# A new hand-written instruction order for a one-core attention and feed-forward kernel

## The chip, the core and the metric

The kernel runs on one core of a Trainium2 chip. The metric is the device time of one execution in microseconds (us). Five instruction streams run side by side and meet only at semaphores: TensorE (matmuls), ScalarE (activations), VectorE, GpSimd, and SyncE, which here only issues DMA transfers.

## The reference

```
xn  = layernorm(x)                      # x: 2048 x 640
q   = (xn @ wq) as 32 heads of 20       # one k and one v head for all
p   = softmax(q k^T / sqrt(20))         # 2048 x 2048 for each head
out = x + (p v) @ wo + silu(xn @ w1) @ w2      # w1: 640 x 1728
```

All inputs and the output are bf16.

## The kernel before

**Tiling.** The 2048 queries are four chunks of 512; the 32 heads are eight groups of four, each head in a strip of 32 partitions. A chunk and a group of heads make one of 32 *groups*, numbered chunk by chunk. In a group, each of 16 key tiles of 128 keys gives four *score blocks* of 128 x 512, one for each head: 2048 blocks in all. A score matmul uses 32 rows of the array, so up to four on different row strips run side by side; such a *score set* takes the time of one matmul. The product with v uses 32 columns for each head: a *value group* is four matmuls of 512 columns side by side.

**Two ways to the exponential.** ScalarE takes a run of one to three neighbouring PSUM banks in one exp (L1258). VectorE takes single blocks: p1 (L1503) turns a score into the bit pattern of an approximate exponential, and two shifted copies of the four blocks of a batch sharpen it, made by GpSimd (L1542) or by VectorE (L1547). A key tile of ScalarE's thus costs one value group, a batch of VectorE's three (all at L1295).

**Dense work.** The projections q, the feed-forward's first layer h (with a tanh on ScalarE, L863, and a product on VectorE, L866), the output jobs ("out", with the second layer and wo) and those of the last chunk ("y", "fin") are jobs of 5 to 19 steps on TensorE (L537, L824), four matmuls side by side in each. Queries are spread into the head strips by small DMAs, the query pieces (L796). When a group ends, its denominators travel through three DMA steps (L938, L943, L946), GpSimd multiplies (L950), and DMAs pack the rows for wo (L963). An output job of a chunk needs the packed rows of all eight groups of it. The h jobs of chunks 2 and 3 need output jobs of chunks 0 and 1 to be done.

**Who sets the order.** The whole program is laid out ahead of time by a planner in the source, class `Sched` with `build`: each operation has an assumed duration and a priority, and `commit` gives it its place on its engine. Up to an assumed 36 us (`HAND`) the planner itself chooses. From there TensorE's order is read from the text `ORDER`, three characters for each step, by `follow`:

- `S`: a score run for ScalarE (banks, first bank); `s` the same, but it begins a new set
- `D`, `E`: one score block for VectorE (batch and head, bank); with `E` the batch's shifts may go to VectorE; `F`, `G` the same, beginning a new set
- `a`, `d`: one value group of a ScalarE tile or of a VectorE batch
- `n`: the first step of a dense job (`q`, `h`, `o`, `y`); `m`: its next step

The texts in `OTHERS` give the order on ScalarE, VectorE and GpSimd, and who goes first at the port which the last two share. SyncE's queue of DMAs is not in them: there the planner takes the transfer with the lowest `prio` among those that it thinks ready. When `ORDER` is used up, the planner goes on by itself. The assumed times set the order only; on the chip each engine runs its list in this order, waiting on semaphores.

## Time and profile before

| | |
|---|---|
| median of three runs | 681.21 us (680.39 to 681.31) |
| profiled execution, its own time | 681.22 us |
| its span, first to last instruction | 679.4 us |
| TensorE busy | 666.0 us, 98% |
| ScalarE busy | 654.4 us, 96% |
| VectorE busy | 632.2 us, 93% |
| GpSimd busy | 514.1 us, 76% |
| mean granted TensorE clock | 0.995 |

Busy times overlap: an instruction's time on an engine runs from its start to its end, and the next may start before that end. Rows by stretch give, for each engine, busy time and in brackets the number of instructions, then the granted clock, the share of the DMA engines and GB/s.

### The profile page before, as it was taken

How to read it: one execution, taken by the hardware profiler on the slowest of the kernel's cores; microseconds unless marked ns; L12 is line 12 of the kernel's file. 1: busy time of each engine (PE TensorE's matmuls, PEld its weight loads, DVE VectorE, ACT ScalarE, POOL GpSimd, SP SyncE). 2: the span in 40 equal slices, each digit the busy share in tenths (PEclk: the TensorE clock that was granted, in tenths of full speed). 3: DMA queues.
4: the chain of work that ended last, by engine and by line, in shares of the span. 5: the costliest groups of instructions: out<-in, count | busy, mean ns of one | idle time of the engine just before them, and what ended most of it. 6: DMA issues, size and time to landing. Idle time of an engine off the chain costs nothing.

```text
span 679.4 us, 22817 instructions
## 1 busy us (share of the span) xinstructions
PE 666.0 (98%) x9898; PEld 240.8 (35%) x9901; DVE 632.2 (93%) x1102; ACT 654.4 (96%) x728; POOL 514.1 (76%) x314
## 2 busy tenths in 40 slices
PE   8999999999999999999999999999999999999998
PEld 5433323332322333333333333333332333333345
DVE  7899999999998999899999999999999899999943
ACT  6999999999998999999999999999999899999992
POOL 6648787878886887876888787788888857777760
PEclk9999999999998999999999999999999899999999
DMA  8652220222221223231212222312222202233201
GB/s 224 184 180 18 32 24 14 27 26 22 34 32 24 32 30 42 29 57 25 23 27 35 36 26 34 40 31 50 21 19 35 25 20 33 31 49 43 23 7 41
DMA packets 34243, 29.00 MB, mean 43 GB/s; under 512 B 15486, under 2 KB 29662, under 8 KB 34142
## 3 DMA queue, kind: packets, MB, share of 16 engines
q1 hardware_dynamic: 33854, 27.20, 25.9%
q8 instruction: 78, 1.28, 0.8%
q10 hardware_dynamic: 288, 0.33, 0.1%
q14 instruction: 23, 0.19, 0.1%
HBM read 11.09 MB, written 2.62 MB: 20 GB/s over the span
## 4 chain that ended last, share of the span: by engine, by line
PE 63%; ACT 20%; DVE 13%; POOL 3%; issue 1%; DMA 0%; POOLq 0%; ACTq 0%
PE psall L1295 21%; PE psall L1168 20%; PE psall L537 20%; ACT sbt L1258 18%; DVE sbt L1503 7%; POOL sbt L1542 3%; ACT sbt L863 1%; DVE sbt L1547 1%; DVE sbt L866 1%; DVE sbt L653 1%; DVE sbt L697 0%; DVE sbt L655 0%; PE psall L711 0%; DVE sbt L783 0%; DVE sbt L1344 0%
## 5 line engine op out<-in xcount | busy, mean ns | idle before, releaser
L1258 ACT ACTIVATE sbt<-psall 128x1024 bf16<-128x1024 f32 (+2 forms) x656 | 624.4, 1067 | 7.1 <-PE psall L1168 5.7
L1542 POOL TENSOR_SCALAR sbt<-sbt 128x2048 int16<-128x2048 int16 x238 | 451.5, 1897 | 112.3 <-PE psall L1295 40.9
L1503 DVE TENSOR_SCALAR sbt<-psall 128x512 int16<-128x512 f32 x712 | 454.6, 682 | 20.3 <-PE psall L1168 15.2
L1295 PE MATMUL psall<-sbt 128*32 128x512 bf16 x3472 | 273.6, 386 | 2.1 <-DVE sbt L1547 0.8
L1168 PE MATMUL psall<-sbt 32*128 32x512 bf16 x2048 | 255.8, 386 | 4.4 <-ACT sbt L1258 1.0
L537 PE MATMUL psall<-sbt 128*32 128x320 bf16 (+3 forms) x3900 | 218.9, 332 | 0.4 <-DVE sbt L1503 0.2
L1168 PEld LDWEIGHTS psall<-sbt 32*128 32x128 bf16 x2048 | 69.3, 91 | 225.6 <-ACT sbt L1258 125.6
L537 PEld LDWEIGHTS psall<-sbt 128*32 128x32 bf16 (+1 forms) x3900 | 84.2, 96 | 86.8 <-issue 46.6
L1295 PEld LDWEIGHTS psall<-sbt 128*32 128x32 bf16 x3472 | 72.8, 95 | 109.2 <-issue 70.6
L1547 DVE TENSOR_SCALAR sbt<-sbt 128x2048 int16<-128x2048 int16 x118 | 80.8, 710 | 0.6 <-PE psall L1295 0.5
L950 POOL TENSOR_TENSOR sbt<-sbt 128x512 bf16<-128x512 f32 x30 | 38.5, 1284 | 20.2 <-DVE sbt L1547 16.8
L866 DVE SCALAR_TENSOR_TENSOR sbt<-sbt,psall 128x512 bf16<-128x512 bf16 x52 | 35.1, 677 | 0.1
L863 ACT ACTIVATE sbt<-psall 128x512 bf16<-128x512 f32 x52 | 32.1, 619 | 0.0
L1344 DVE COPY sbt<-psall 128x512 f32<-128x512 f32 x31 | 21.1, 681 | 0.4 <-PE psall L1295 0.3
L783 DVE TENSOR_SCALAR sbt<-psall 128x512 bf16<-128x512 f32 x20 | 13.6, 678 | 0.1
L1009 DVE SCALAR_TENSOR_TENSOR sbt<-psall,sbt 128x320 f32<-128x320 f32 x8 | 3.9, 486 | 10.2 <-PE psall L537 10.2
L662 POOL TENSOR_TENSOR sbt<-sbt 128x2 f32<-128x2 f32 x8 | 5.7, 708 | 8.5 <-DVE sbt L660 8.2
L993 DVE SCALAR_TENSOR_TENSOR sbt<-psall,sbt 128x320 bf16<-128x320 f32 x24 | 11.6, 485 | 0.2 <-PE psall L537 0.2
L675 POOL TENSOR_SCALAR sbt<-sbt 128x640 bf16<-128x640 bf16 x12 | 10.4, 874 | 1.5 <-DVE sbt L667 1.5
L653 DVE BATCH_NORM_STATS2 sbt<-sbt 128x6 f32<-128x320 bf16 x14 | 6.6, 472 | 1.9 <-DMA sbt<-in_A_x_dram 1.9
L685 PE MATMUL psall<-sbt 128*128 128x128 bf16 x80 | 6.9, 220 | 1.5 <-DVE sbt L678 1.5
L1824 PE MATMUL psall<-sbt 128*32 128x256 bf16 x144 | 6.5, 338 | 1.2 <-DVE sbt L577 1.2
(63 smaller groups left out, 98.8 us busy)
## 6 DMA issues: line engine op xcount, KB each, us to landing
sbt<-sbt SPq DMA_DIRECT2D x120, 64.0 KB, 3.8
sbt<-in_A_x_dram SPq DMA_DIRECT2D x28, 160.0 KB, 4.1
sbt<-sbt SPq DMA_DIRECT2D x213, 20.0 KB
out_dram<-sbt SPq DMA_DIRECT2D x14, 160.0 KB, 2.1
sbt<-in_B_w_dram SPq DMA_DIRECT2D x1, 2160.0 KB, 13.9
sbt<-in_B_w_dram SPq DMA_DIRECT2D x1, 2080.0 KB, 8.4
sbt<-sbt SPq DMA_DIRECT2D x75, 8.0 KB
sbt<-in_A_wq_dram SPq DMA_DIRECT2D x1, 800.0 KB, 5.8
```

What stands on the lines that cost most here:

```text
L537: ins = pe.matmul(ps[j * SLOT:(j + 1) * SLOT, b * BANK + off:b * BANK + off + n], w[:, j * SLOT:(j + 1) * SLOT], x, start=start, stop=stop ...
L783: op = Op("dve", lambda v: v.tensor_scalar_mul(q_st[:, st, :], bk(job.bank), QSCALE), t_dve(512), DVE_END, pre=[job.ready], writes=[res("q ...
L863: t = Op("act", lambda a: a.activation(t_buf[0:rows, ts, :], bk(job.bank, 0, QW, rows=rows), AF.Tanh, scale=0.5), t_act(512), ACT_END, pre ...
L866: u = Op("dve", lambda v: v.scalar_tensor_tensor(out=hT[par][0:rows, fk, :], in0=t_buf[0:rows, ts, :], scalar=1.0, in1=bk(job.bank, 0, QW, ...
L950: nm = pool(lambda e: e.tensor_tensor(oU[:, us, :], U_sb[:, us, :], Rrep, ALU.mult), 1356.0, POOL_END, pre=[uc] + lc + pack_op.get(divmod( ...
L1168: return pe.matmul(bk(b), kT_rep[i * SLOT:(i + 1) * SLOT, kt * P:(kt + 1) * P], qT[i * SLOT:(i + 1) * SLOT, g % NQ, :], start=True, stop=T ...
L1258: return a.activation(Ebuf[:, es * QW:es * QW + w], ps[:, buf[0] * BANK:buf[0] * BANK + w], AF.Exp, scale=ESCALE)
L1295: ins = pe.matmul(ps[i * SLOT:(i + 1) * SLOT, ub * BANK:ub * BANK + QW], lhsT, rhs, start=(first and k < HG), stop=(last and k >= len(lst) ...
L1344: return v.tensor_copy(U_sb[:, us, :], bk(ub))
L1503: p1 = Op("dve", lambda v: v.tensor_scalar(z16[:, i * QW:(i + 1) * QW], bk(job.bank), ZBIAS, 0.0, ALU.add, ALU.max), t_dve(QW) + 2.0, DVE_ ...
L1542: op = pool(lambda v, t=t, j=j, zin=zin: v.tensor_scalar(t.bitcast(I16), zin, float(SHIFT[j]), 1.0, ALU.add, ALU.mult), POOL_SHIFT, POOL_E ...
L1547: op = dve(lambda v, t=t, j=j, zin=zin: v.tensor_scalar_add(t.bitcast(I16), zin, float(SHIFT[j])), t_dve(N, 4), prio=SPRIO - 0.01 * j, **args)
```

## The change

`ORDER` and the four texts of `OTHERS` are replaced as a whole. `ORDER` grows from 3046 to 3153 entries and reaches further into the program's end. Packed rows get a lower priority number in SyncE's queue. Three assumed durations of `make_sel`, which writes constants for the end of the program, are changed. An `S` entry can name banks with a step of two.

```diff
 ORDER = (
-    "D32D13S14a97nq6m00m00D25S20Dd2m00m00S23nh5aa7S20D66m00D32D03S14m00m00m00S20S12Dd6ab7nh4m00m00m00m00S20D33D05nh6m00m00m00m00nh2S20D23Dd4m00m00m00m00ac7"
...
-    "d94d84ny2m00m00S25E37m00S20Dc3m00da4d74dc4S35D33m00m00m00m00a54S10E21m00a64S35D33m00m00m00m00db4S20D13m00m00m00S25D87a74a84S30E23a94df4S35")
+    "D32D13S14a97nq6m00m00D25S20m00m00S22D34aa7S20Dd5nh6m00D04D22S13m00m00m00S20S14Dd5G33nh2m00m00m00m00S25D00D31nh4m00m00m00m00ab7S25D20S13nh2m00m00m00m00"
...
+    "S24D83m00m00m00dd7de7a00S31a10m00m00S24D17m00m00m00m00m00m00S21D33m00a20S24D27m00a30m00d00S31d30d10d60a40S35a50a60d20S31d40a70S35S14d50d70d90d80a80da0"
+    "S31db0S35")
...
                 o = dma(f"pk{us}", lambda e, c=c, r=r, n=n, lo=lo: e.dma_start(oT[r:r + n, par, c, :], oU[lo:lo + n, us, :]),
-                        n * QW * 2 + 200000, pre=[nm] + ([kT_op[k] for k in range(KT)] + q_op[0] if qc == 1 else []), reads=[res("oU", us)], writes=[res("oT", par, gi, i, c)], prio=0.6)
+                        n * QW * 2 + 200000, pre=[nm] + ([kT_op[k] for k in range(KT)] + q_op[0] if qc == 1 else []), reads=[res("oU", us)], writes=[res("oT", par, gi, i, c)], prio=0.45)
...
-        a = pool(lambda g: g.memset(qT[:, 2, :], 0.0), 300, writes=q_res[NGR - NQ] + [res("sel")], prio=0.91)
+        a = pool(lambda g: g.memset(qT[:, 2, :], 0.0), 1067, writes=q_res[NGR - NQ] + [res("sel")], prio=0.91)
...
         if k == "S":
-            op = make_s_act(tuple(range(b, b + int(a))))
+            d, n = divmod(int(a, 36), 4)
+            op = make_s_act(tuple(range(b, b + (n or 4) * (d + 1), d + 1))[:n or 4])
             what = ("s", None)
```

The two other durations of `make_sel` go from 180 to 193 and from 280 to 292. For reference, query pieces have `prio=0.55` and the three denominator steps `prio=0.5`.

## The prediction

> **What bounds the kernel now.** I read the page first, then the busy time by stretch, the groups by form, and the timelines of single engines.

> ```profile
> PE 666.0 (98%) x9898; PEld 240.8 (35%) x9901; DVE 632.2 (93%) x1102; ACT 654.4 (96%) x728; POOL 514.1 (76%) x314
> PE 63%; ACT 20%; DVE 13%; POOL 3%; issue 1%; DMA 0%; POOLq 0%; ACTq 0%
> 36.80:176.00 139.20, 138.50 (x1852) 44.47 (x1848) 137.45 (x232) 138.98 (x168) 110.76 (x61) 1.00 0.24 35
> 176.00:216.00 40.00, 37.39 (x430) 11.21 (x426) 38.52 (x63) 37.98 (x40) 32.49 (x18) 0.96 0.25 33
> 216.00:516.00 300.00, 299.16 (x4520) 104.00 (x4516) 289.48 (x485) 299.19 (x337) 239.99 (x133) 1.00 0.25 32
> 516.00:536.00 20.00, 18.50 (x213) 5.62 (x209) 18.15 (x31) 17.97 (x20) 17.57 (x13) 0.91 0.25 31
> 664.20:679.40 15.20, 11.88 (x315) 8.46 (x311) 5.64 (x11) 3.26 (x4) 0.00 (x0) 1.00 0.14 46
> ```

> Two engines bound it together: from 36.8 us on, TensorE and ScalarE are both busy for nearly the whole of most stretches (299.16 and 299.19 of 300 us), and DMA has 0% of the chain that ended last. The stretches 176 to 216 and 516 to 536 stand out: there both lose time, and the granted clock falls below 1. The opening up to 36.8 us is not in the hand-written order and stays.

> TensorE's prices come from its timeline (start, duration, then the matmuls):

> ```profile
> 565.52 0.39 PE L1168 MATMUL psall<-sbt 32*128 32x512 bf16 x3
> 565.84 0.40 PE L1295 MATMUL psall<-sbt 128*32 128x512 bf16 x4
> 566.17 0.39 PE L1168 MATMUL psall<-sbt 32*128 32x512 bf16 x3
> 566.50 0.73 PE L537 MATMUL psall<-sbt 128*32 128x320 bf16 x16
> 567.05 0.39 PE L1295 MATMUL psall<-sbt 128*32 128x512 bf16 x4
> 569.78 0.83 PE L1295 MATMUL psall<-sbt 128*32 128x512 bf16 x12
> 570.54 0.39 PE L1168 MATMUL psall<-sbt 32*128 32x512 bf16 x3
> ```

> Starts count, not durations. Four groups of 320 columns take 566.50 to 567.05, 0.136 each. A score set (L1168) followed by a value group (L1295) takes 0.32, and so does the way back, 0.33. Three value groups and one way back take 0.76 (569.78 to 570.54). From the last two, two more value groups cost 0.43, so 0.216 each, and a change between score and other work costs 0.105 on top, in either direction. There are no gaps: with the order given, TensorE's time is a sum of these.

> ScalarE likewise:

> ```profile
> L1258 ACT ACTIVATE sbt<-psall 128x1024 bf16<-128x1024 f32 x520 | 494.9, 1049 | 6.6 <-PE psall L1168 5.7
> L1258 ACT ACTIVATE sbt<-psall 128x1536 bf16<-128x1536 f32 x80 | 116.1, 1485 | 0.2
> L1258 ACT ACTIVATE sbt<-psall 128x512 bf16<-128x512 f32 x56 | 34.8, 632 | 0.3
> 311.68 1.49 ACT L1258 ACTIVATE sbt<-psall 128x1536 bf16<-128x1536 f32 x1
> 313.01 0.65 ACT L863 ACTIVATE sbt<-psall 128x512 bf16<-128x512 f32 x1
> 313.49 2.00 ACT L1258 ACTIVATE sbt<-psall 128x512 bf16<-128x512 f32 x2
> ```

> From start to start, three banks take 1.33 us and one bank 0.48; two banks lie between, an estimate of 0.905. Every exp thus carries about 0.05 us beside its elements.

> **The clock.** These windows of 3.41 us are laid on the two half-clock periods:

> ```profile
> 185.53:188.94 3.41, 2.93 (x26) 0.97 (x26) 3.41 (x7) 3.41 (x5) 2.97 (x3) 1.00 0.59 66
> 206.02:209.43 3.41, 2.23 (x21) 0.58 (x21) 3.41 (x5) 3.41 (x4) 1.56 (x1) 1.00 0.11 27
> 209.43:212.84 3.41, 3.35 (x31) 0.71 (x31) 2.64 (x5) 1.67 (x2) 2.57 (x2) 0.50 0.10 24
> 526.87:530.28 3.41, 2.33 (x25) 0.65 (x24) 3.40 (x6) 3.41 (x4) 3.12 (x3) 1.00 0.10 24
> 530.28:533.70 3.42, 3.42 (x34) 1.04 (x34) 1.71 (x3) 1.62 (x3) 3.18 (x4) 0.50 0.07 14
> ```

> In each half-clock window TensorE is busy throughout and ScalarE falls to 1.67 and 1.62 us: it loses 1.74 and 1.80 us, and TensorE half of 3.4. I take 1.75 us a period. The window ahead of each held the fewest matmuls of the steady part (x21, x25); a window of x26 passed. Every matmul here covers a quarter of the array, so the count is a measure of array work. I read it so: a sparse window halves the next one's clock. The sparse places are the two in which no dense work is to be had: after the last q and h job of one query chunk, until its output jobs may start. [...]

> **The change, part by part.** The order is a text of three-character entries; I count them by kind in its old and new form.

> ```profile
> L1295 PE MATMUL psall<-sbt 128*32 128x512 bf16 x3472 | 273.6, 386 | 2.1 <-DVE sbt L1547 0.8
> L1503 DVE TENSOR_SCALAR sbt<-psall 128x512 int16<-128x512 f32 x712 | 454.6, 682 | 20.3 <-PE psall L1168 15.2
> L1542 POOL TENSOR_SCALAR sbt<-sbt 128x2048 int16<-128x2048 int16 x238 | 451.5, 1897 | 112.3 <-PE psall L1295 40.9
> ```

> Score blocks: 2048 in all. The old order places 1255 in S entries and 705 in D and E entries, and leaves 88 to the opening and the planner's own end; the new places 1286 and 712, leaving 50, which is just the opening's share (46 and 4). So the new order runs to the last score block. VectorE now gets 716 blocks, 179 batches, against 712 (L1503 above), 178; ScalarE gets 1332 against 1336.

> *TensorE.* A batch adds two value groups: 868 (3472 by 4) become 870, +0.43 us. Walking the entries with the rule that neighbouring score blocks on different row groups share one set, I find 608 sets after the opening against 613, -1.08, and some 12 fewer changes between score and other work (about 1145 against 1157), -1.26. Dense jobs are the same. Sum -1.9 us, of some 640.

> *ScalarE.* Runs of one, two and three banks: 56, 520, 80 become 80, 506, 80. That is 24 x 0.48 - 14 x 0.905 = -1.2 us.

> *VectorE and GpSimd.* Four more p1 of 0.682 and two fewer shifts there; GpSimd four more shifts of 1.897, +7.6 us. Both are under 97% in 216 to 516, so I cost them at nothing; without that cover GpSimd's 7.6 would lie open.

> *Where dense work stands.* In the first sparse place the old order has two q jobs (10 groups, 40 matmuls) between the end of group 6 and the first output job, the new one (20): thinner. In the second, after group 23, the old has two q jobs; the new opens six h jobs in group 24, drawn from groups 21 and 22. Laying the entries along ScalarE's prices, I find the old order's sparse windows at about 187, 205 and 525 us, as the trace has them, and in the new one only the one near 205 falls under 24 matmuls a window. So the second half-clock period should go, -1.75 us; the first stays, or is missed if the windows fall otherwise (another -1.75).

> *The DMA queue.* Packed rows get priority 0.45 in place of 0.6: ahead of query pieces (0.55) and of the denominator's transfers (0.5), where both are ready.

> ```profile
> 185.34 6.75 SPq L796 DMA_DIRECT2D sbt<-sbt  x9
> 192.14 0.71 SPq L963 DMA_DIRECT2D sbt<-sbt  x1
> POOL sbt L950 <- DMA sbt<-sbt: 2.3, 3, 1.6
> ```

> Here packs (L963) do follow nine query pieces (L796). But the first output matmul comes only at about 213 us, and query pieces are placed several groups ahead of their first score, so either can slip by these 6.75 us unseen. The longest wait of the multiply on a transfer is 1.6 us. I cost the queue at 0, with bounds of -2.3 (all of that wait) and +2.3. The three changed durations of make_sel and the two-step stride of an S entry move nothing themselves; no S entry of the new order uses a stride.

> *The end.*

> ```profile
> 639.46 27.34 ACT L1258 ACTIVATE sbt<-psall 128x1024 bf16<-128x1024 f32 x23
> 667.08 2.07 PE L537 MATMUL psall<-sbt 128*32 128x320 bf16 x56
> 669.08 1.05 PE L1089 MATMUL psall<-sbt 128*128 128x4 f32 x8
> 670.97 5.11 PE L537 MATMUL psall<-sbt 128*32 128x128 bf16 x144
> ```

> The last exp ends at 666.80; from there 12.6 us pass, 2.07 of them on y jobs left over and about four on the parts of the last projection that need not wait. The new order has all y jobs placed before the last score set, and the early parts can run under the last exps. From the exps' side that saves up to 2.1 us; from TensorE's side nothing, for the same work is only moved, and the sums of group 30, earlier spread among score sets, now lie there too. I take 0, with -2.1 and +2 (the wait for the last exps lying open, about one run and a half of 1.33) as ends.

> *Sum.* Other waits, for which I have no ground to expect a change, are carried over. TensorE: -1.9 - 1.75 = -3.65; ScalarE: -1.2 - 1.75 - up to 2.1 = -5.05. The slower of the two counts. The profiled execution took 681.22 us around a span of 679.4 (1.8 outside it); the median is 681.21, so nothing is to be shifted. 681.2 - 3.65 is 677.6; with an even chance that the first half-clock period is missed too I lower it by a part of that, to **677.2 us**. This case alone: 675 to 679.

> **The rivals.** *The end eats it.* The cover of y jobs is gone, TensorE stands in wait of the last exps (+2 us) and the sparse places give two periods again: 681.2 - 1.9 + 2 = 681.3, no change. For it: the last entries are long runs on ScalarE with little between them. Against: the last projection's early parts are there to fill.

> *Short runs starve ScalarE: slower.* The 24 further one-bank runs give TensorE 0.48 us to bring the next score set, less than a change to other work and back with one group in between (0.32 + 0.33).

> ```profile
> 294.52 1.10 ACT L1258 ACTIVATE sbt<-psall 128x512 bf16<-128x512 f32 x2
> 295.74 0.60 ACT L1258 ACTIVATE sbt<-psall 128x512 bf16<-128x512 f32 x1
> ```

> Here two one-bank exps took 1.22 us from start to start of the third, where 0.96 would do: 0.26 lost. If every added one lost that, 24 x 0.26 = 6.2: 677.2 + 6.2 = 683.4. It decides from 0.22 us each. For it: the trace's own example, and 0.621 busy for each (34.8 by 56). Against: most one-bank runs stand ahead of a tanh of an h job, which fills the time.

> *The clock is no matter of sparse windows.* Then two periods stay: 681.2 - 1.9 = 679.3, still faster, by little.

> *The change does only half of what it says,* the queue's new priority moving nothing that anyone waits for: I hold this true, and it is in the sum.

> **How the numbers follow.** Forecast 0.56; end eats it 0.13; short runs or like waits in TensorE's fixed order 0.17; clock unchanged 0.10; better than the forecast, both periods gone and the end's 2.1 saved (673.8), 0.04. A measurement of this kernel can tell 0.2%, 1.4 us, from no change: faster means under 679.8, slower over 682.6. The forecast, the better case and most of the clock case are faster: 0.69; same 0.14; slower 0.17. The range, 673.8 to 682.5, leaves out most of the slower rival and little else.

> **What would show it.** Right: 870 value groups; exps 80, 506, 80; one half-clock period or none, none near 530; no y matmul after the last exp; matmul starts still 0.32 apart at each change. Wrong: two or more half-clock periods, or new ones; ScalarE below 99% in 216 to 516 with waits on L1168; more than 12.6 us from the last exp to the end; a TensorE wait on a transfer.

## The result, and the profile after

The changed kernel takes 675.01 us in the median of four runs (674.64 to 675.24); the kernel before took 680.8 us beside it (678.86 to 681.31). The ratio is 0.992, with a 95% interval of 0.9899 to 0.9941. The profiled execution of the changed kernel took 674.64 us around a span of 672.8 us, 6.6 us less than the span of 679.4 us before. Its line numbers are three higher: the exp is L1261, value groups are L1298, score matmuls L1171, p1 L1506, GpSimd's shift L1545, dense steps L540, packs L966.

From the page of the changed kernel, busy times and the chain by engine:

```profile
PE 662.0 (98%) x9911; PEld 241.6 (36%) x9911; DVE 628.5 (93%) x1102; ACT 653.1 (97%) x738; POOL 525.2 (78%) x320
PE 85%; DVE 10%; ACT 3%; issue 1%; POOL 1%; DMA 0%; DVEq 0%; ACTq 0%
```

The same stretches, by the view of windows (busy time and count for TensorE, its weight loads, VectorE, ScalarE and GpSimd; then granted clock, DMA share, GB/s):

```profile
36.80:176.00 139.20, 138.76 (x1858) 44.91 (x1854) 138.16 (x234) 139.11 (x173) 112.65 (x62) 1.00 0.24 35
176.00:216.00 40.00, 37.66 (x466) 11.96 (x465) 39.73 (x68) 40.00 (x41) 32.64 (x19) 1.00 0.26 32
216.00:516.00 300.00, 299.53 (x4512) 104.44 (x4512) 291.59 (x491) 299.58 (x337) 249.30 (x137) 1.00 0.27 34
516.00:536.00 20.00, 19.77 (x298) 6.72 (x294) 19.35 (x33) 19.76 (x24) 18.35 (x13) 1.00 0.16 17
```

The clock is 1.00 in every one: the two half-clock periods are both gone from this execution, and the other three have a mean clock of 0.999 or 1.0 too. ScalarE is busy for 40.00 us of 176 to 216, where it had 37.98, and for 19.76 of 516 to 536, where it had 17.97. In 216 to 516 it stays full. TensorE now holds 85% of the chain that ended last, where it had 63% and ScalarE 20%.

The groups by form show that the order says what was read from its text:

```profile
L1261 ACT ACTIVATE sbt<-psall 128x1024 bf16<-128x1024 f32 x506 | 483.0, 1061 | 2.3 <-PE psall L1171 1.9
L1545 POOL TENSOR_SCALAR sbt<-sbt 128x2048 int16<-128x2048 int16 x244 | 462.9, 1897 | 97.2 <-DVE sbt L1550 36.8 <-PE psall L1298 22.4 <-PE psall L1171 9.8
L1506 DVE TENSOR_SCALAR sbt<-psall 128x512 int16<-128x512 f32 x716 | 454.8, 681 | 21.0 <-PE psall L1171 16.9
L1298 PE MATMUL psall<-sbt 128*32 128x512 bf16 x3480 | 272.9, 384 | 1.4 <-POOL sbt L1545 1.1
L1261 ACT ACTIVATE sbt<-psall 128x1536 bf16<-128x1536 f32 x80 | 116.7, 1474 | 0.9 <-PE psall L1171 0.4
L1261 ACT ACTIVATE sbt<-psall 128x512 bf16<-128x512 f32 x80 | 49.2, 633 | 0.3 <-PE psall L1171 0.2
```

3480 matmuls make 870 value groups; the exps are 80, 506 and 80. ScalarE's waits at the three forms add to 3.5 us; they were 7.1 (6.6, 0.2 and 0.3).

The end, from the timelines of ScalarE and TensorE (start, duration, then what ran):

```profile
654.53 7.31 ACT L1261 ACTIVATE sbt<-psall 128x1536 bf16<-128x1536 f32 x6
...
661.89 0.40 PE L1298 MATMUL psall<-sbt 128*32 128x512 bf16 x4
662.12 0.40 PE L540 MATMUL psall<-sbt 128*32 128x128 bf16 x16
662.78 1.05 PE L1092 MATMUL psall<-sbt 128*128 128x4 f32 x8 [0.26 <-ACT sbt L1399]
664.66 4.88 PE L540 MATMUL psall<-sbt 128*32 128x128 bf16 x128
```

The last exp ends at 661.84, 10.96 us ahead of the end; before it was 12.6 us. The 2.07 us of y steps that lay there are gone, and only 16 of the last projection's 144 matmuls run ahead of the last sum.

### The profile page after: what moved, and what is told of

The parts are those of the page before. It is cut to its first block, busy times and chain, and to the rows that moved or that the text cites. A ratio compares the mean times of both kernels' runs of the same rounds, so it can differ in the third digit from the quotient of the medians.

```text
span 672.8 us, 22813 instructions
## 1 busy us (share of the span) xinstructions
PE 662.0 (98%) x9911; PEld 241.6 (36%) x9911; DVE 628.5 (93%) x1102; ACT 653.1 (97%) x738; POOL 525.2 (78%) x320
## 4 chain that ended last, share of the span: by engine, by line
PE 85%; DVE 10%; ACT 3%; issue 1%; POOL 1%; DMA 0%; DVEq 0%; ACTq 0%
PE psall L1298 29%; PE psall L1171 28%; PE psall L540 25%; DVE sbt L1506 7%; ACT sbt L1261 2%; DVE sbt L1550 1%; PE psall L714 1%; PE psall L688 1%; DVE sbt L869 0%; PE psall L827 0%; DVE sbt L1347 0%; DMA sbt<-in_A_x_dram 0%; PE psall L1110 0%; POOL sbt L1545 0%; DVE sbt L786 0%
## 5 line engine op out<-in xcount | busy, mean ns | idle before, releaser
L1261 ACT ACTIVATE sbt<-psall 128x1024 bf16<-128x1024 f32 (+2 forms) x666 | 624.4, 1059 | 3.5 <-PE psall L1171 2.5
L1545 POOL TENSOR_SCALAR sbt<-sbt 128x2048 int16<-128x2048 int16 x244 | 462.9, 1897 | 97.2 <-DVE sbt L1550 36.8
L1506 DVE TENSOR_SCALAR sbt<-psall 128x512 int16<-128x512 f32 x716 | 454.8, 681 | 21.0 <-PE psall L1171 16.9
L1298 PE MATMUL psall<-sbt 128*32 128x512 bf16 x3480 | 272.9, 384 | 1.4 <-POOL sbt L1545 1.1
L1171 PE MATMUL psall<-sbt 32*128 32x512 bf16 x2048 | 252.0, 384 | 3.1 <-DVE sbt L1506 0.9
L540 PE MATMUL psall<-sbt 128*32 128x320 bf16 (+3 forms) x3904 | 218.6, 331 | 0.1
L1171 PEld LDWEIGHTS psall<-sbt 32*128 32x128 bf16 x2048 | 70.0, 91 | 222.2 <-ACT sbt L1261 122.6
L540 PEld LDWEIGHTS psall<-sbt 128*32 128x32 bf16 (+1 forms) x3904 | 84.5, 95 | 81.0 <-issue 40.8
L1298 PEld LDWEIGHTS psall<-sbt 128*32 128x32 bf16 x3480 | 71.7, 94 | 111.4 <-issue 73.2
L1550 DVE TENSOR_SCALAR sbt<-sbt 128x2048 int16<-128x2048 int16 x114 | 76.0, 698 | 0.0
```

The lines of the kernel that those rows point to most:

```text
L540: ins = pe.matmul(ps[j * SLOT:(j + 1) * SLOT, b * BANK + off:b * BANK + off + n], w[:, j * SLOT:(j + 1) * SLOT], x, start=start, stop=stop ...
L1171: return pe.matmul(bk(b), kT_rep[i * SLOT:(i + 1) * SLOT, kt * P:(kt + 1) * P], qT[i * SLOT:(i + 1) * SLOT, g % NQ, :], start=True, stop=T ...
L1261: return a.activation(Ebuf[:, es * QW:es * QW + w], ps[:, buf[0] * BANK:buf[0] * BANK + w], AF.Exp, scale=ESCALE)
L1298: ins = pe.matmul(ps[i * SLOT:(i + 1) * SLOT, ub * BANK:ub * BANK + QW], lhsT, rhs, start=(first and k < HG), stop=(last and k >= len(lst) ...
L1506: p1 = Op("dve", lambda v: v.tensor_scalar(z16[:, i * QW:(i + 1) * QW], bk(job.bank), ZBIAS, 0.0, ALU.add, ALU.max), t_dve(QW) + 2.0, DVE_ ...
L1545: op = pool(lambda v, t=t, j=j, zin=zin: v.tensor_scalar(t.bitcast(I16), zin, float(SHIFT[j]), 1.0, ALU.add, ALU.mult), POOL_SHIFT, POOL_E ...
```

## The experiments

In the comparisons below, the *progress* of two executions is the difference of their times at the start of every 64th of the 2048 score matmuls. It shows at which place one kernel falls behind another. A *zero group* has the form of a value group, with zero weights; here some are put into `ORDER` by a new entry `z`. They add nothing to the result and give TensorE work where it would wait. Times on different chips differ (the kernel before has a median of 681.05 us on one and of 679.7 to 679.8 on three others), so each kernel has a ratio to the kernel before on its own chip.

### The clock in the old order

```diff
+        elif k == "z":
+            op, what = filler(999.0), ("fill", None)
...
-    "...S21D34D20a53S26Dc5de3..."
+    "...S21D34D20z00a53S26Dc5z00de3..."
```

**fill_second**, the old order with 11 zero groups near 519 to 530 us:

> The old order with 11 value groups of zeros added on TensorE between about 519 and 530 us, where it waits. Sparse-window theory: no half-clock period near 530 us any more, one near 209 may stay; the 2.4 us of added matmuls lie in waits of 2.8 us, so the time falls by about 1.5 us against the old order (1 to 2), where that has both periods. Rival, the clock does not depend on how sparse TensorE's work is: the period near 530 us stays, and the time is the same or up to 2.4 us longer.

681.3 us, ratio 0.9996 (0.9986 to 1.0005): the gain of 1 to 2 us did not come. The profiled execution has one half-clock period, at 210.2 us, and a span of 679.3; five of the eleven executions have a mean clock of 0.994 or 0.995, which is two periods, so that the second one is gone in the profile and not in all of them. **fill_both**, 28 zero groups at both places:

> The old order with zero groups at both sparse places, 11 there and 17 more between about 184 and 210 us: 6.0 us of added matmuls. Sparse-window theory: no half-clock period at all, clock 1.00, and about 3.2 us less than the old order with two periods (2.5 to 3.8), so 677.4 to 678.7; the new order is still faster by 2.3 to 3.5 us, by its fewer sets and changes. Rival, no dependence: two periods stay, and 0 to 6 us more.

680.63 us, ratio 1.0003 (0.9991 to 1.0015); no half-clock period, clock 1.00, and a span of 678.2. In the profiles the periods go where the zero groups are put, but the gain does not show in the time. In fill_both 1.1 us are lost against fill_free (below), which has fewer groups: 0.64 at the first place and about as much at the second; its zero groups also move entries of VectorE's list from 215 us on and of GpSimd's from 530 us on, since the planner gives them a duration. fill_second gains 0.97 us at the second place against the kernel before, but it is 0.65 us late at the first, where it has no zero group and the same lists: that is a difference between executions, and part of it is a wait of 0.36 us for VectorE at 191.93. **fill_few** has only 16 (its expectation and the next say 15), ahead of the longer waits:

> The old order with 15 zero groups in place of 28, only ahead of waits of about 0.28 us and more (nine at the first sparse place, six at the second): 3.2 us of added matmuls. Theory that each half-clock period costs about 1.75 us and that the zero groups which stood ahead of no wait hid this: no period or one, and 1.5 to 3.5 us less than the old order. Rival, a period costs little because the engines around it are waiting anyway: within 0.8 us of the old order.

679.2 us, ratio 0.999 (0.9981 to 0.9999), span 677.9, no period; near 365 to 383 us it loses 0.8 to 1.0 us against fill_free, which lacks the wait of 0.95 us on a DMA that TensorE has there. **fill_free** has the same ones, with no assumed duration, so that all other engines' lists stay:

```diff
             op, what = filler(999.0), ("fill", None)
+            op.occ = 0.0
```

> The old order with the same 15 zero groups as fill_few, counted by the order's own model as taking no time, so that the lists of VectorE, ScalarE, GpSimd and the DMA queue are those of the kernel before, place for place, and only TensorE has more to do, in its waits. Theory that a stretch in which TensorE's array does too little work halves the clock that follows: no half-clock period or one, a span of 676.5 to 677.9 us, a median 1.5 to 3 us under the kernel before. Rival, that the halving costs nothing because TensorE then catches up in its waits: within 0.8 us of the kernel before.

678.74 us (678.45 to 679.78), ratio 0.9987 (0.9978 to 0.9996); no half-clock period, span 677.0. **old_again**, the kernel before unchanged:

> The kernel before, unchanged, in another execution: a profile to set beside the first one. Theory that its sparse stretches near 203 and 523 us halve the clock whenever a whole window of 3.41 us falls on them: the number of half-clock periods differs between executions (none to two), and each one less is worth 1 to 1.8 us of the span. Rival, that the periods belong to the order and not to where the windows fall: two periods again, at the same places, and a span within 0.5 us of 679.4.

680.41 us (679.11 to 681.92), ratio 1.0013 (1.0003 to 1.0022), span 678.2. The windows of this second execution of the same program, at the two sparse places:

```profile
206.29:209.70 3.41, 2.17 (x25) 0.62 (x26) 3.41 (x5) 3.41 (x4) 1.50 (x1) 1.00 0.10 25
209.70:213.12 3.42, 3.42 (x31) 0.68 (x23) 2.77 (x5) 1.59 (x2) 2.79 (x2) 0.50 0.10 24
527.12:530.53 3.41, 2.40 (x27) 0.75 (x27) 3.10 (x6) 3.26 (x4) 3.12 (x4) 1.00 0.10 25
530.53:533.95 3.42, 3.42 (x65) 1.40 (x61) 3.25 (x6) 2.99 (x4) 3.27 (x3) 1.00 0.04 8
```

The second place passes at full clock. The program is the same; the window lies 0.25 us later and catches 27 matmuls instead of 25. The two executions run level up to 523 us (within 0.1 us) and differ by 1.21 us from 563 us on. From two profiles of one program this gives a price of one period: 1.21 us. In fill_free the same windows hold more work:

```profile
205.49:208.91 3.42, 2.92 (x38) 0.88 (x36) 3.42 (x6) 3.42 (x4) 1.71 (x2) 1.00 0.16 32
526.27:529.68 3.41, 3.19 (x40) 1.10 (x40) 3.41 (x6) 3.41 (x5) 3.07 (x4) 1.00 0.12 30
```

It is 1.12 us ahead of old_again from the first place on, and keeps that at the second, which old_again passes at full clock (-1.14 at 640 us). So in these profiles a period costs 1.1 to 1.2 us, and the old order without any has a span of 677.0.

The medians alone can't tell this: old_again is the same program as the kernel before and still comes out at 1.0013 (1.0003 to 1.0022), as far from 1 as fill_free on the other side, and the forecast of 1.5 to 3 us for fill_free's median is missed. But the mean granted clock of every execution is on record, and one window at half clock takes 0.0025 off it (half of 3.41 us in 679): the profile of old_again, with one, has 0.997, that of the kernel before, with two, 0.995, and that of thin_first, with three, 0.992. Of 90 executions of the kernel before in these runs, six are at 0.998 or more; of the 33 of fill_both, fill_few and fill_free, all are. On the three chips of fill_few, fill_free and fill_wait, the kernel before takes in the mean 678.9 us with no period (clock 0.999 or 1.0), 679.7 with one (0.997), 680.6 with two (0.995 or 0.994) and 681.3 with three (0.992), in 6, 44, 12 and 4 executions; three at 0.996 are left out. That is 0.8 us for each period. old_order_new_queue, below, is the exception: its two executions without a period are no faster than the four with one. On fill_free's chip the two executions of the kernel before without a period took 678.63 and 679.0 us, and fill_free 678.74. So a period costs about 0.8 to 1.2 us, and the old order's usual case is one, not two. The rival of "within 0.8" is not excluded by the median (1.0 us less, 0.3 to 1.5); the rival that the periods belong to the order falls with old_again.

### The clock in the new order

**thin_first** makes the new order sparse at the first place:

```diff
+    def thin(g, kt):
+        return g == 8 and 6 <= kt <= 11
...
-            return pv_mms(pe, flags["bank"], lst, flags["first"], flags["last"])
+            return pv_mms(pe, flags["bank"], lst, flags["first"], flags["last"], 64 if thin(g, kt) else QW)
```

> The new order with less work: the ten value groups of key tiles 6 to 11 in group 8 multiply 64 of their 512 columns only, about 1.9 us less on TensorE near 201 to 208 us (this part of the product with v is left out). Sparse-window theory: a half-clock period appears there, and the time rises by 1 to 2 us over the new order's 675.0 although there is less to do. Rival, no dependence: no such period, and 0 to 1.9 us less.

677.09 us, ratio 0.9942 (0.9926 to 0.9958), span 675.0; the five executions have two or three half-clock windows by their mean clock. The windows of the profile:

```profile
200.90:204.31 3.41, 2.65 (x31) 0.85 (x31) 3.41 (x7) 3.41 (x5) 3.33 (x2) 1.00 0.70 59
204.31:207.73 3.42, 2.65 (x35) 0.84 (x34) 3.42 (x7) 3.36 (x5) 2.05 (x2) 0.50 0.37 43
207.73:211.14 3.41, 3.41 (x26) 0.61 (x26) 2.80 (x5) 2.93 (x3) 2.75 (x2) 0.50 0.04 8
211.14:214.55 3.41, 3.41 (x31) 0.65 (x31) 2.16 (x4) 2.38 (x3) 3.25 (x3) 0.50 0.08 19
```

About 1.9 us less work (an estimate: ten groups of 448 columns fewer, at 0.216 us for 512) makes the program 2.2 us later than the changed kernel (2.1 in the medians), all of it at this place, with three windows at half clock. The changed kernel passes this place, in its own windows, with

```profile
203.41:206.82 3.41, 2.65 (x30) 0.78 (x30) 3.41 (x7) 3.41 (x5) 2.94 (x2) 1.00 0.64 79
```

and no half clock behind it. TensorE's busy time is the same 2.65 us and ScalarE is full in both; what differs is the columns that the matmuls stream. So here the half clock came behind a window in which TensorE was busy for 2.65 of 3.41 us, and it was the kernel with less array work that had it.

### Order and queue apart

The two parts of the change were run singly, each a single number in the packs' line:

```diff
-... prio=0.45)
+... prio=0.6)
```

**new_order_old_queue** is the changed kernel with 0.6:

> The new order with the packed rows' priority back at 0.6. TensorE, ScalarE and GpSimd have the same lists; only SyncE's queue and the place of the reciprocals on VectorE differ. Theory that nobody waits for this queue: 675.0 within 0.7 us, the same as the changed kernel. Rival, the queue brings part of the gain: 676.5 or more, with TensorE or GpSimd waits on a transfer that the changed kernel lacks.

678.43 us, ratio 0.996 (0.9946 to 0.9974), span 677.5. The expectation is missed by 3.4 us. The queue's own timeline in this kernel:

```profile
361.26 8.07 SPq L799 DMA_DIRECT2D sbt<-sbt  x10
369.38 0.60 SPq L941 DMA_DIRECT2D sbt<-sbt  x1
370.02 2.94 SPq L799 DMA_DIRECT2D sbt<-sbt  x4
373.01 1.47 SPq L966 DMA_DIRECT2D sbt<-sbt  x2
374.52 0.62 SPq L946 DMA_DIRECT2D sbt<-sbt  x1
375.19 1.46 SPq L966 DMA_DIRECT2D sbt<-sbt  x2
```

and in the changed kernel:

```profile
360.25 6.26 SPq L799 DMA_DIRECT2D sbt<-sbt  x8
366.56 3.18 SPq L966 DMA_DIRECT2D sbt<-sbt  x4
```

The four packs (L966) are issued by 369.74 in the one and by 376.65 in the other, 6.9 us later, behind six more query pieces and two denominator steps. An output job is waiting for them by then. Level until 360 us but for 1.0 us, most of it from the first sparse place, this kernel falls 3.6 us further behind the changed one between 360 and 379 us. **old_queue_again** is the same text on another chip, and **fill_wait** puts nine zero groups into the wait and moves nothing else:

```diff
-    "...S20D84S15m00m00m00m00m00a33..."
+    "...S20D84S15m00m00m00m00z00z00z00z00z00z00z00z00z00m00a33..."
```

> The same text as new_order_old_queue, on the same chip as fill_wait, so that the two can be compared. About 678.4 us; a wait of 2.2 us on a DMA near 376 us and a half-clock period behind it. If the wait is a matter of where transfers fall in one execution and not of the order of the queue, it is absent or much shorter here and the time is nearer 675.

> The new order under the old queue priority, as in new_order_old_queue, with nine zero groups (36 matmuls of 512 columns that add nothing, about 1.9 us) placed ahead of the one group of an output job on which TensorE there stood 2.18 us for a DMA; no other instruction of any engine moves. Theory that the late packed row costs twice, once by the wait and once by the half clock after the sparse window that the wait makes: the half-clock period near 380 us goes, the multiply's progress is 1.1 to 1.6 us ahead of old_queue_again behind 385 us, and the median is as much lower; the wait itself stays. Rival, that the half clock costs nothing beside the wait, or that it comes from something else at that place: within 0.5 us of old_queue_again.

old_queue_again takes 678.67 us (677.21 to 679.33), ratio 0.9979 (0.997 to 0.9988), span 676.9; fill_wait 677.57 us (677.4 to 678.04), ratio 0.9968 (0.9955 to 0.998), span 675.7. The clock of the single executions says the same within one program: the three of old_queue_again at 0.999 or 1.0 took 677.21 to 677.6 us, the other eight, at 0.996 or 0.997, 678.49 to 679.33; all five of fill_wait are at 1.0. TensorE's timeline in old_queue_again:

```profile
375.00 0.73 PE L540 MATMUL psall<-sbt 128*32 128x320 bf16 x16
377.70 0.32 PE L540 MATMUL psall<-sbt 128*32 128x320 bf16 x4 [1.97 <-DMA sbt<-sbt]
```

and its windows:

```profile
374.49:377.90 3.41, 1.44 (x36) 0.58 (x28) 1.23 (x2) 2.10 (x4) 3.23 (x2) 1.00 0.21 29
377.90:381.32 3.42, 3.42 (x33) 0.58 (x29) 2.10 (x4) 1.86 (x3) 0.57 (x1) 0.50 0.89 67
```

The same two views of fill_wait:

```profile
375.15 0.73 PE L540 MATMUL psall<-sbt 128*32 128x320 bf16 x16
375.70 2.12 PE L1827 MATMUL psall<-sbt 128*32 128x512 bf16 x36
377.74 0.32 PE L540 MATMUL psall<-sbt 128*32 128x320 bf16 x4
```

```profile
374.49:377.90 3.41, 3.41 (x76) 1.55 (x64) 1.38 (x3) 2.25 (x4) 3.08 (x2) 1.00 0.30 35
377.90:381.32 3.42, 3.34 (x49) 1.01 (x45) 3.18 (x6) 2.62 (x3) 0.75 (x2) 1.00 0.83 67
```

The pack lands no earlier (the group that needs it starts at 377.74 and 377.70), but the window behind the wait keeps its clock (1.00, against 0.50), and fill_wait gains 1.3 us there (progress from +0.15 to -1.13), 1.1 us in the median. So the late packs cost about 3.4 us at this place in old_queue_again: 2 us of waiting (1.97) and 1.3 of half clock, which was gone when the wait was filled; little of that is made up later.

**old_order_new_queue** is the kernel before with 0.45:

> The old order with the packed rows' priority at 0.45. Theory: the old order leaves enough room for its packs, so the priority alone gives nothing: the old order's time within 0.7 us. Rival, the queue is itself worth time: 1 us or more less than the old order.

681.89 us, ratio 1.0032 (1.002 to 1.0043): neither the theory nor the rival. It is slower by about 2 us, though its profile has no half-clock period; its span is 679.9, 2.9 us over fill_free. In the waits of GpSimd on a DMA the row that stood at 2.3 us is now

```profile
POOL sbt L950 <- DMA sbt<-sbt: 5.9, 4, 4.3
```

and the longest wait, 4.28 us, ends at 210.36, where the same multiply started at 207.31 in the kernel before. Its four denominator transfers are issued at 203.51 instead of 200.39: the packs' priority rearranges the queue in a way for which the old order had not been chosen. GpSimd's next shift starts at 211.72 instead of 210.19, and at 218.57 TensorE has stood 1.08 us for the eviction of an output job. Of the loss against fill_free, 1.4 us arise between 203 and 224 us and 2.35 by 639 us; what makes the later part is open.

**new_again**, the changed kernel on that chip:

> The changed kernel itself, beside the others on the same chip. 675.0 within 0.7 us, clock 1.00.

675.2 us, ratio 0.9935 (0.9923 to 0.9947), span 673.0. The four cases, as ratios to the kernel before: old order and old queue 1, old order and new queue 1.0032, new order and old queue 0.996 and 0.9979 on two chips, both new 0.992 and 0.9935 in two measurements. The last two cases were not measured side by side.

### Does TensorE's count matter?

**fill_dense**, the new order with 19 zero groups between value groups where TensorE never waits:

> The new order with 19 zero groups spread over 228 to 498 us, between value groups where TensorE does not wait: 4.1 us more on TensorE, nothing on any other engine. If TensorE's list sets the time, +3.5 to +4.1 us, and the 2.3 us that the new order saves there count in full. If ScalarE sets it as much as TensorE, under +2 us. If ScalarE alone, under +0.7.

678.23 us against 675.2 of new_again, and a span of 676.8 against 673.0. Of 4.1 us of further work (19 by 0.216) 3.0 us appear in the median and 3.8 in the span, with the clock at 1.00. The span is within the first case's bounds; the median lies between the first case and the second. These zero groups have an assumed duration, so some entries of VectorE's list move too, from 294 us on. Of what was added to TensorE's list here, three quarters or more came out in the time.

## Why the prediction was right, and where it was not

The forecast was 677.2 us, with 675 to 679 for its likeliest case. The result of 675.01 us is at the edge of that case and 2.2 us below the forecast.

*TensorE's count: right as far as it can be read.* The groups, runs and blocks are as counted (870; 80, 506, 80; 716 for VectorE; GpSimd's shifts 244, where 242 was said). In the traces the changes between score and other work go from 1161 to 1145, sixteen fewer where twelve were said. The sets, 613 and 608 in the prediction, can't be told apart in a trace, which doesn't name the row strips. With them as said and the prices of the prediction that is -2.3 us, where -1.9 was said. fill_dense shows that most of such a term counts.

*The clock: reading borne out, price and number off.* In these runs the half clock follows sparse windows, none of them idle: TensorE was busy for 2.23 and 2.33 of 3.41 us ahead of the two periods of the kernel before. thin_first makes such a period (0.50 behind 2.65 us), and fill_wait removes one (1.00 behind 3.41 us, where old_queue_again has 0.50 behind 1.44). But the price taken, 1.75 us (ScalarE's loss within the window), was too high: 0.8 to 1.2 us in the old order, 1.3 at the wait of old_queue_again, as if part were made up behind it. The number was off too: the sum had one period and a part of another, and none is left in eight of nine executions of the changed kernel (the ninth has a mean clock of 0.997 and 676.39 us). In the profile two periods at 1.2 give 2.4 us, where the sum had 1.75 and about 0.4: the two errors nearly cancel, and that was luck. The reading that the first place is thinner in the new order did not hold either, for its thinnest window has 30 matmuls there, not under 24, and the one behind it ran at 1.00. The even chance for the first period supposed that windows can fall otherwise on the same program; no trace showed that then, old_again does, with 0.25 us at the second place. And the base was a matter of chance: the profiled execution before had two periods, the usual one has one, and a kernel without any is only 1.0 us below the median.

*The DMA queue: wrong.* The step "I cost the queue at 0", with the case that the new priority moves nothing anyone waits for held true, failed. It looked at the one place where packs follow nine query pieces in the old order, and found slack there. But the slack belongs to the old order. In the new one the old priority costs about 3 us (0.996 against 0.992, and 0.9979 against 0.9935, of 680 us: 2.7 and 3.0; paired the other way, 1.7 and 4.0), mostly by a wait of 2 us and the half clock behind it (about 1.3 us in old_queue_again); in the old order the new priority costs about 2 us. The total did not suffer, because the sum compared old with new as wholes, and in the profiles of these two TensorE does not wait for a pack: the term came out right for a reason that the prediction did not have.

*The end: between its bounds, and not settled.* 0 was taken, with -2.1 as one bound. On ScalarE it went nearly to that bound: from the last exp to the end are 10.96 us instead of 12.6, 1.6 us less, by the 2.07 us of y steps that the prediction named. On TensorE the y steps moved ahead of the last score set, as said, and its idle time did not shrink: behind its last score matmul it is idle for 3.7 of 14.1 us, in fill_free for 3.3 of 15.2.

*What makes the 4.2 us* between fill_free (span 677.0, old order without half clock) and the changed kernel (672.8): on ScalarE, 1.2 us of runs (as predicted), 1.6 us of the end, and 0.9 us less waiting at its exps (in fill_free 3.8, 0.3 and 0.3), 3.7 in all. On TensorE, 2.3 us of count; where the other 1.9 come from is not shown. Progress can't tell, because the two orders place the same score matmul differently: between 84 and 662 us it wanders from 1.7 us behind to 7.1 ahead, with 2.4 ahead at 640 us and 3.1 at the last score matmul. Which of the two engines sets each microsecond was not separated, nor was a kernel run that changes the end alone.

*The rivals.* The end ate nothing. The short runs did not starve ScalarE: its one-bank exps stand idle 0.3 us in all, as before, with 24 more of them. "The clock is no matter of sparse windows" falls with thin_first and fill_wait, and with the executions without a period of fill_both, fill_few and fill_free.

## What to carry to other kernels

An order written for fixed queues must be judged together with them: the same priority number was worth about 3 us under one order and cost 2 under another, so the slack that a trace shows belongs to that trace's order alone. A wait on the matmul engine, here of about 2 us, is to be priced with what the clock does behind it, here another 1.3 us; filling it with useless matmuls got that part back in fill_wait. Before a stall of one profile enters a sum, a second profile of the same program, or the mean clock of its other executions, shows whether it is always there.

## What the runs showed of the hardware

In thin_first three windows in a row ran at half clock (10.24 us), although TensorE was busy for 3.41 us of the second of them. Why the third one still did is not shown.
